# Top-k attention and a cosine-gated feed-forward on one core: four weight chunks in each of the first units, some in other buffers, and twelve units instead of eight transposed by TensorE

## The chip, the core and the metric

The kernel runs on one core of a Trainium2 chip. The metric is the device time of one execution in microseconds; three executions of the kernel before took 1467.22, 1468.61 and 1470.07 us. The core has five engines with a queue of instructions each: TensorE (PE in the profile; PEld are its weight loads), VectorE (DVE), ScalarE (ACT), GpSimd (POOL) and SyncE (SP), which only issues DMAs here. They wait for each other by semaphores.

## The reference

```python
# q, k, v: (8, 8, 576, 64): 8 batches, 8 heads
scores = 0.125 * q @ k.T
kth = np.partition(scores, -32, axis=-1)[..., -32:-31]
scores = np.where(scores >= kth, scores, -1e9)
attn = softmax(scores)              # the sum has 1e-9 added
x = (attn @ v).transpose(0, 2, 1, 3).reshape(4608, 512)
h = x @ w_in                        # (512, 2048)
return (h * np.cos(h)) @ w_out      # (2048, 512)
```

Both weight matrices arrive as 64-bit floats.

## The kernel before

**Units.** The 4608 tokens are cut into 36 blocks of 128; a block with two heads is a unit, so that there are 144 units, four to a block. Where a block spans two batches its units have two parts. For each unit, TensorE makes the scores of 128 queries against 576 keys for two heads (`scores`, L223); ScalarE copies them into SBUF (`take_scores`, L233 and L234). VectorE finds the 32 largest of each row: it folds the row into 288 larger values (`fold_high`, L244) and 288 lesser ones, and searches both with MAX8 and MATCH_REPLACE8 (L349, L354) in four rounds, of which the fourth takes the lesser values too (`topk_round`). The lesser values come from VectorE at once (`fold_now`, L252) in units up to number `EARLY`, and from two integer operations of GpSimd (`fold_sum` L262, `fold_low` L271) after it. From the bound found, ScalarE masks (`mask`, L378 and L380) and exponentiates with row sums (`exponentials`, L388); VectorE adds and inverts the sums (`sums` and `reciprocal`, L396 and L401; the tiles `den` and `rden`).

**Two ways to transpose.** The weights of attention must be transposed before they meet `v`. In early units GpSimd normalises them (`normalise`, L409), TensorE transposes them in nine pieces (`transposes_now`, tile `tp`), ScalarE copies the result into `pT`, TensorE multiplies with `v` (`values`, L474) and ScalarE copies the product into the block's `xT` (`take_values`, L485). In paired units GpSimd splits the words into 16-bit halves (`split`, L421 and L423), SP writes them to HBM and reads them back through a transposing DMA, and VectorE normalises the product (L483) two units at a time.

**Feed-forward.** When a block's four units are done, eight steps `ff1` (L534) multiply its `xT` by `w_in`; ScalarE evacuates each bank of two steps twice (`take_first`, L548 and L550), GpSimd and ScalarE make the cosine (L570, L579, and `sines`, L589, whose function and that of the exponentials need different tables, so that a table load stands at each change), GpSimd multiplies (`gate`, L596), and eight steps `ff2` (L609) multiply by `w_out`. `feed(n)` puts up to n such steps into TensorE's order, under a credit of five a slot less 0.9 for each unit whose scores are made there. There are 576 steps in all.

**Weights.** They are loaded in 32 chunks of 512 KB and converted to 32-bit floats in three stages: `decode_first` on ScalarE (L128), `decode_second` on GpSimd (L138) and VectorE (L141), `decode_third` on GpSimd (L151). Chunks are staged in seven buffers with the tag `g`, which the feed-forward's gates use too; the four buffers with the tag `x` belong to the sines.

**The order.** It is written out by hand: one slot for each unit, in which the functions are called in a fixed order, and each call appends instructions to the queues of its engines. Slots up to `EARLY` = 8 are `early_slot`, then come `slot` and, for the last units, `last_slot`. In slot i, VectorE searches unit i, the mask, exponentials and transposes are of unit i - 1, and scores are made ahead. The early slot reads the sums in its third round, the other in its fourth:

```python
        decode_second(n)                  # early_slot
        topk_round(u, 2, both(w))
        topk_round(u, 3)
        if w:
            normalise(w)
...
        decode_second(2)                  # slot
        topk_round(u, 3, both(w), z)
```

Of the kernel before, what the change touches and what calls it, by code (L numbers as in the profile page):

```python
# [11 lines left out]
I32 = mybir.dt.int32  # L12
# [5 lines left out]
P = 128  # L18
# [12 lines left out]
def kernel(  # L31
# [16 lines left out]
    NP = H // 2  # L48
# [12 lines left out]
    ffw = ctx.enter_context(tc.tile_pool(name="ffw", bufs=2))  # L61
# [13 lines left out]
    CW = 512  # L75
# [8 lines left out]
    for i in range(DF // CW):  # L84
        w = consts.tile([P, NC, CW], F32, tag=f"w_in{i}", name=f"w_in{i}")
# [4 lines left out]
    for f in range(NF):  # L90
        w = consts.tile([P, DM], F32, tag=f"w_out{f}", name=f"w_out{f}")
        w_out.append(w)
        chunks.append((moe_w_out[f * P : (f + 1) * P, :], w))
    CHUNKS, XB = 7, 4
    ff = {"live": 0, "tick": 0, "now": 0, "credit": 0.0, "end": False, "kind": 0, "half": 0, "open": 0}

    wq = {"next": 0, "loaded": deque(), "second": deque(), "third": deque(), "done": 0, "ready": 0}

    def staged():
        return sum(len(wq[k]) for k in ("loaded", "second", "third"))  # L100

    def load_weights(n):
        for _ in range(n):
            i = wq["next"]
            if i >= len(chunks):
                return
            src, dst = chunks[i]
            if not DECODE:
                nc.sync.dma_start(out=dst, in_=src)
                wq["next"] = wq["done"] = i + 1  # L110
                continue
            if staged() + ff["live"] >= CHUNKS:
                return
            st = ffw.tile([P, CW, 2], I32, tag="g", name="st", bufs=CHUNKS)
            nc.sync.dma_start(out=st.rearrange("p w i -> p (w i)"), in_=src)
            wq["loaded"].append((st, dst))
            wq["next"] = i + 1


# [2 lines left out]
    def decode_first(n):  # L122


        for _ in range(min(n, len(wq["loaded"]))):
            st, w = wq["loaded"].popleft()
            hi = st[:, :, 1]
            nc.scalar.activation(  # L128
                out=w, in_=hi.bitcast(F32), func=AF.Prelu, scale=2.0**-111, alpha=2.0**32
            )  # L130
            wq["second"].append((st, w))

    def decode_second(n):

        for _ in range(min(n, len(wq["second"]))):
            st, w = wq["second"].popleft()
            wi, lo = w.bitcast(I32), st[:, :, 0]
            nc.gpsimd.tensor_scalar(  # L138
                out=lo, in0=lo.bitcast(U32), scalar1=2.0**-29, scalar2=1.0, op0=ALU.mult, op1=ALU.mult
            )  # L140
            nc.vector.tensor_scalar(  # L141
                out=wi, in0=wi, scalar1=3, scalar2=None, op0=ALU.logical_shift_left
            )
            wq["third"].append((st, w))

    def decode_third():

        while wq["third"]:
            st, w = wq["third"].popleft()
            wi = w.bitcast(I32)  # L150
            nc.gpsimd.tensor_tensor(out=wi, in0=wi, in1=st[:, :, 0], op=ALU.add)  # L151
            wq["done"] += 1
# [16 lines left out]
    NU = len(units)  # L169
# [68 lines left out]
    def fold_high(u):  # L238

        s, sc = u["s"], u["sc"]  # L240
        if u["n"] > EARLY:
            del u["sc"]
        u["rest"] = work.tile([P, 2, S], F32, tag="rest", name="rest", bufs=1)
        nc.vector.tensor_tensor(  # L244
            out=u["rest"][:, :, HS:S], in0=sc[:, :, 0:HS], in1=s[:, :, HS:S], op=ALU.max
        )
# [9 lines left out]
    def fold_sum(u):  # L256

        if not u["folds"]:
            return
        s = u["s"].bitcast(I32)  # L260
        u["low"] = work.tile([P, 2, HS], F32, tag="low", name="low", bufs=1)
        nc.gpsimd.tensor_tensor(  # L262
            out=u["low"].bitcast(I32), in0=s[:, :, 0:HS], in1=s[:, :, HS:S], op=ALU.add
        )

    def fold_low(u):

        if not u["folds"]:
            return
        low = u["low"].bitcast(I32)  # L270
        nc.gpsimd.tensor_tensor(  # L271
            out=low, in0=low, in1=u["rest"][:, :, HS:S].bitcast(I32), op=ALU.subtract
        )
# [15 lines left out]
    def topk_first(u, w):  # L289

        u["top"] = tops[u["n"] % len(tops)]
        merges = w and w["folds"]
        if merges:
            merge_first(w)
        if u["folds"]:
            if u["n"] > EARLY:
                fold_sum(u)
            fold_high(u)
        else:
            u["rest"] = work.tile([P, 2, S], F32, tag="rest", name="rest", bufs=1)  # L300
        if merges:
            merge_second(w)
        if u["folds"] and u["n"] <= EARLY:
            fold_now(u)
        topk_round(u, 0, [lambda: bounds(w), lambda: distances(w)] if w else ())

# [27 lines left out]
    def merge_first(u):  # L334
        n = TOPK // 2 + 1
        u["lesser"] = u["top"].rearrange("p j r i -> p j (r i)")[:, :, 2 * n : 3 * n]
        nc.vector.tensor_reduce(
            out=u["lesser"], in_=u["top"][:, :, 0:n], axis=mybir.AxisListType.X, op=ALU.min
        )

    def merge_second(u):
        nc.vector.tensor_reduce(
            out=u["top"][:, :, TOPK - 1, 1], in_=u.pop("lesser"), axis=mybir.AxisListType.X,
            op=ALU.max,
        )
# [57 lines left out]
    def both(u):  # L403
        return [lambda: sums(u), lambda: reciprocal(u)] if u else ()
# [88 lines left out]
    for w in widths:  # L493
# [10 lines left out]
    second = deque(  # L504
        (blk, i, f) for blk in blocks for i in range(blk["w"] // P) for f in range(0, NF, 2)
    )
# [159 lines left out]

    EARLY, LAST = 2 * NP, NU - NP
    scored, last, last_values = {}, {}, {}  # L670
    for i, u in enumerate(units):
        two = i % 2 == 0 and EARLY + 2 < i < LAST + 2 and (len(u["parts"]) == 1 or u["hp"] == 0)
# [4 lines left out]
    at_slot = {}  # L677
    order = [(b, hp) for b in range(B) for hp in range(NP)]
    for n in range(NP, len(order)):
        i = last[order[n - 5]] if n >= 5 else 0  # L680
        at_slot.setdefault(max(i, NP + 2), []).append((load_qk, *order[n]))
        i = last_values[order[n - 6]] if n >= 6 else 0
        at_slot.setdefault(max(i + 4 - i % 2, NP + 2), []).append((load_v, *order[n]))

    for hp in range(NP):
        at_slot.setdefault(hp, []).append((load_v, 0, hp))
# [7 lines left out]
        u["paired"] = EARLY <= i < LAST  # L694

    def early_slot(i, u, w):
        n = 3 if i < 6 else 2
        topk_first(u, w)
        if i == 0:
            decode_second(1)  # L700
        scores(units[i + 1])
        for load, b, hp in at_slot.get(i, []):
            load(b, hp)
        load_weights(n)
        if w:
            mask(w)
            exponentials(w)
        topk_round(u, 1)

        decode_second(n)  # L710
# [4 lines that stand above are left out]
        take_banks()  # L715
        take_scores(units[i + 1])
        gate(1)
        decode_third()
        feed(2)
        reduce_first()  # L720
        reduce_second()
        if i != NP:
            decode_first(n - 1)
        if w:
            transposes_now(w)
        feed(1)
        decode_first(n - len(wq["second"]))
        if w:
            values([w])
            take_values([w])  # L730
        feed(2)
        sines(2)

    def send(x):

        split(x)
        write_halves(x)
        transposes(x)

    def slot(i, u, w, x, z):  # L740
        load_weights(2)
        if x:
            send(x)
        topk_first(u, w)
        fold_low(u)
        topk_round(u, 1)
        topk_round(u, 2)
        made = scored.get(i, [])
        if z:
            take_banks()  # L750
        feed(1)

        for m in made:
            scores(m)
        if z:
            values(z)


        late = len(made) > 0

        decoding = i < EARLY + 8
        if i % 2 and not decoding:
            sines(1)
        if w:
            mask(w)
        take_banks()
        if w and late:
            exponentials(w)
        take_scores(units[i + 1])
        if w and not late:  # L770
            exponentials(w)
        decode_second(2)
        topk_round(u, 3, both(w), z)
        for load, b, hp in at_slot.get(i, []):
            load(b, hp)
        gate(1)
        feed(1 if len(made) == 2 else 2)
        take_banks()
        decode_third()
        decode_first(2)  # L780
        reduce_first()
        reduce_second()
        feed(1 if len(made) == 2 else 3)
        if decoding or i == LAST:
            sines(1)
# [50 lines left out]
    for i in range(NU + 1):  # L836
# [4 lines left out]
        u, w = (units[i - n] if 0 <= i - n < NU else None for n in range(2))  # L841
        x = units[i - 2] if EARLY <= i - 2 < LAST else None
# [54 lines left out]
```

## Time and profile before

| | |
|---|---|
| median of three runs | 1468.61 us |
| the profiled execution | 1468.61 us, of which its span is 1466.8 us |
| granted TensorE clock, mean | 0.97 |
| busy: PE, DVE, ACT, POOL | 1404.1, 1365.5, 1078.5, 1160.0 us |
| start of slots 0, 9, 13, 22 (their L244) | 7.38, 108.29, 153.79, 242.49 us |
| moved by DMA | 229.53 MB, mean 156 GB/s |

A slot is counted from the start of its L244 on VectorE. From slot 22 two slots take 18.69 us; in slots 2 to 5 one takes 10.8 us. Busy times of TensorE are modelled, and a busy share is a mean over stages. Idle time of an engine that isn't the bound in its stage costs nothing by itself. The granted clock is 0.5 in stretches of the first 167 us and 1.0 from there to the end.

### The profile page before, as it was taken

How to read it: one execution, taken by the hardware profiler on the slowest of the kernel's cores; microseconds unless marked ns; L12 is line 12 of the kernel's file. 1: busy time of each engine (PE TensorE's matmuls, PEld its weight loads, DVE VectorE, ACT ScalarE, POOL GpSimd, SP SyncE). 2: the span in 40 equal slices, each digit the busy share in tenths (PEclk: the TensorE clock that was granted, in tenths of full speed). 3: DMA queues.
4: the chain of work that ended last, by engine and by line, in shares of the span. 5: the costliest groups of instructions: out<-in, count | busy, mean ns of one | idle time of the engine just before them, and what ended most of it. 6: DMA issues, size and time to landing. Idle time of an engine off the chain costs nothing.

```text
span 1466.8 us, 30361 instructions
## 1 busy us (share of the span) xinstructions
PE 1404.1 (96%) x10360; PEld 1012.0 (69%) x10360; DVE 1365.5 (93%) x5209; ACT 1078.5 (74%) x1908; POOL 1160.0 (79%) x836
## 2 busy tenths in 40 slices
PE   4778899999999999999999999999999999999998
PEld 3566567777777767777777767777677777777765
DVE  7999999999999999999999999999999999999831
ACT  4667677777777777777777777777777787777651
POOL 4679888888888887888888888888888888888410
PEclk6578999999999999999999999999999999999999
DMA  8434576666665566557665667666766566655200
GB/s 279 152 101 130 151 199 175 159 162 174 184 166 151 152 186 180 167 145 180 192 167 146 150 172 193 168 151 162 192 179 152 149 161 175 168 151 147 67 8 15
DMA packets 405547, 229.53 MB, mean 156 GB/s; under 512 B 355088, under 2 KB 371728, under 8 KB 405392
## 3 DMA queue, kind: packets, MB, share of 16 engines
q1 hardware_dynamic: 399984, 217.93, 56.3%
q10 hardware_dynamic: 5408, 9.65, 1.8%
q8 instruction: 82, 1.34, 0.4%
q14 instruction: 73, 0.60, 0.1%
HBM read 45.09 MB, written 95.94 MB: 96 GB/s over the span
## 4 chain that ended last, share of the span: by engine, by line
PE 84%; DVE 7%; ACT 5%; DMA 2%; POOL 1%; issue 1%; SPq 0%; ACTq 0%; POOLq 0%
PE mm L534 31%; PE o L609 31%; PE rim L474 11%; PE sc L223 7%; DVE top L349 3%; PE rim L223 2%; DVE rest L354 2%; ACT s L388 1%; ACT s L380 1%; PE tp L448 1%; DMA st<-in_moe_w_in_dram 1%; ACT s L233 1%; ACT L388 1%; DMA v<-in_v_dram 0%; DVE w_out L141 0%
## 5 line engine op out<-in xcount | busy, mean ns | idle before, releaser
L534 PEld LDWEIGHTS mm<-xT,w_in 128*128 128x128 f32 x4608 | 537.1, 192 | 68.7 <-issue 65.7
L609 PE MATMUL o<-w_out,g 128*128 128x512 f32 x1152 | 541.8, 604 | 11.4 <-POOL g L596 8.7
L534 PE MATMUL mm<-xT,w_in 128*128 128x128 f32 x4608 | 539.7, 275 | 1.1 <-DVE xT L483 0.8
L349 DVE MAX8 top<-rest 128x8 f32<-128x288 f32 x1148 | 481.3, 454 | 0.0
L421 POOL COPY halves<-s 128x2304 uint16<-128x2304 uint16 x132 | 277.7, 2104 | 150.2 <-ACT s L388 147.0
L354 DVE MATCH_REPLACE8 rest<-top,rest 128x288 f32<-128x288 f32 (+1 forms) x860 | 377.0, 446 | 0.0
L609 PEld LDWEIGHTS o<-w_out,g 128*128 128x128 f32 x1152 | 203.8, 192 | 201.3 <-issue 187.0
L349 DVE MAX8 top<-low 128x8 f32<-128x288 f32 x568 | 239.3, 448 | 2.7 <-POOL low L271 2.7
L388 ACT ACTIVATE s<-s,nd 128x576 f32<-128x576 f32 x288 | 220.1, 766 | 0.8
L380 ACT ACTIVATE s<-s,top 128x576 f32<-128x576 f32 x288 | 206.1, 766 | 0.0
L271 POOL TENSOR_TENSOR low<-low,rest 128x576 int32<-128x576 int32 x133 | 187.9, 1413 | 10.4
L262 POOL TENSOR_TENSOR low<-s 128x576 int32<-128x576 int32 x133 | 187.8, 1412 | 1.3 <-DVE rden L401 1.3
L548 ACT ACTIVATE g<-mm 128x512 f32<-128x512 f32 x144 | 85.8, 596 | 130.5 <-PE mm L534 126.4
L474 PE MATMUL rim<-pT,v 128*64 128x128 f32 (+1 forms) x2560 | 161.9, 271 | 8.6 <-ACT pT L455 8.0
L579 POOL TENSOR_TENSOR x<-g,x 128x1024 f32<-128x1024 f32 x68 | 160.9, 2366 | 5.7
L596 POOL TENSOR_TENSOR g<-g,x 128x1024 f32<-128x1024 f32 x68 | 161.4, 2374 | 2.6 <-ACT x L589 2.5
L223 PE MATMUL sc<-k,q 64*128 64x448 f32 (+1 forms) x640 | 155.3, 589 | 8.3 <-DMA k<-in_k_dram 8.3
L474 PEld LDWEIGHTS rim<-pT,v 128*64 128x64 f32 x2560 | 134.3, 140 | 20.4 <-ACT pT L455 10.4
L233 ACT COPY s<-sc 128x896 f32<-128x896 f32 x144 | 129.2, 897 | 4.5 <-PE sc L223 4.1
L354 DVE MATCH_REPLACE8 low<-top,low 128x288 f32<-128x288 f32 x284 | 123.5, 442 | 0.0
L234 ACT COPY s<-rim 128x256 f32<-128x256 f32 x144 | 55.0, 382 | 87.4 <-PE rim L474 87.4
L244 DVE TENSOR_TENSOR rest<-sc,s 128x576 f32<-128x576 f32 x142 | 106.2, 748 | 6.6 <-ACT s L234 6.6
(59 smaller groups left out, 1325.6 us busy)
## 6 DMA issues: line engine op xcount, KB each, us to landing
rows<-halves SPq DMA_DIRECT2D x132, 640.0 KB, 3.0
out_dram<-ob ACTq DMA_DIRECT2D x36, 256.0 KB, 2.1
q<-in_q_dram SPq DMA_DIRECT2D x31, 288.0 KB, 3.8
st<-in_moe_w_in_dram SPq DMA_DIRECT2D x16, 512.0 KB, 5.6
v<-in_v_dram SPq DMA_DIRECT2D x32, 256.0 KB, 3.3
st<-in_moe_w_out_dram SPq DMA_DIRECT2D x16, 512.0 KB, 4.1
k<-in_k_dram SPq DMA_DIRECT2D x31, 144.0 KB, 3.7
k<-in_k_dram SPq DMA_DIRECT2D x32, 128.0 KB, 3.8
```

What stands on the lines that cost most here:

```text
L223: nc.tensor.matmul(to[r0 : r0 + rows, j, 0 : k1 - k0], st["q"][d, q0 : q0 + rows], st["k"][d, k0:k1], start=True, stop=True,)
L262: nc.gpsimd.tensor_tensor(out=u["low"].bitcast(I32), in0=s[:, :, 0:HS], in1=s[:, :, HS:S], op=ALU.add)
L271: nc.gpsimd.tensor_tensor(out=low, in0=low, in1=u["rest"][:, :, HS:S].bitcast(I32), op=ALU.subtract)
L349: nc.vector.max(to[:, j], src[:, j])
L354: nc.vector.match_replace(rest[:, j], to[:, j], src[:, j], NEG)
L380: nc.scalar.activation(out=s[:, j], in_=s[:, j], func=AF.Prelu, bias=less[:, j, 1:2], scale=1.0, alpha=FAR)
L388: nc.scalar.activation(out=s[:, j], in_=s[:, j], func=AF.Exp, bias=nd[:, j : j + 1], scale=SCALE, accum_out=den[:, j, 0:1],)
L421: nc.gpsimd.tensor_copy(out=halves[:, :, 0 : 2 * S], in_=s.rearrange("p (k h) -> p h k", h=2))
L474: nc.tensor.matmul(o[d, to], lhsT, rhs, start=c == 0, stop=c == NT)
L534: nc.tensor.matmul(mm[:, at : at + w], w_in[f // FC][:, c, (f % FC) * P : (f % FC + 1) * P], blk["xT"][:, c], start=c == 0, stop=c == NC - 1,)
L596: eng.tensor_tensor(out=g, in0=g, in1=x, op=ALU.mult)
L609: nc.tensor.matmul(o, g[:, at : at + P], w_out[f], start=f == 0, stop=f == NF - 1)
```

## The change

An early slot handles four weight chunks in slots 0 to 7 and two after them, instead of three up to slot 5. A chunk with an odd number among the first twelve is staged in a buffer of the sines' tag `x`, up to four at a time; the limit of seven on the others counts only those with the tag `g`. `EARLY` is 12 instead of 8, so slots 9 to 12 become early slots, and units 8 to 11 are normalised by GpSimd and transposed by TensorE. A new name, `DECODING` = 8, keeps the old place for what else hung on `EARLY`: units up to number 8 have their lesser values from VectorE, those after it from GpSimd. The first loads of the second batch move from slot 6 to slot 10. The slots in which the sines stand at the end of `slot` are now those before 14 instead of 16.

```diff
-    def staged():
-        return sum(len(wq[k]) for k in ("loaded", "second", "third"))
+    def staged(spare=0):
+        return sum(c[2] == spare for k in ("loaded", "second", "third") for c in wq[k])
...
-            if staged() + ff["live"] >= CHUNKS:
+            spare = i < 3 * XB and i % 2 == 1 and staged(1) < XB
+            if spare:
+                st = ffw.tile([P, CW, 2], I32, tag="x", name="st", bufs=XB)
+            elif staged() + ff["live"] >= CHUNKS:
                 return
-            st = ffw.tile([P, CW, 2], I32, tag="g", name="st", bufs=CHUNKS)
+            else:
+                st = ffw.tile([P, CW, 2], I32, tag="g", name="st", bufs=CHUNKS)
             nc.sync.dma_start(out=st.rearrange("p w i -> p (w i)"), in_=src)
-            wq["loaded"].append((st, dst))
+            wq["loaded"].append((st, dst, int(spare)))
...
-        if u["n"] > EARLY:
+        if u["n"] > DECODING:
             del u["sc"]
...
-            if u["n"] > EARLY:
+            if u["n"] > DECODING:
                 fold_sum(u)
...
-        if u["folds"] and u["n"] <= EARLY:
+        if u["folds"] and u["n"] <= DECODING:
             fold_now(u)
...
-    EARLY, LAST = 2 * NP, NU - NP
+    EARLY, LAST, DECODING = 3 * NP, NU - NP, 2 * NP
...
-        at_slot.setdefault(max(i, NP + 2), []).append((load_qk, *order[n]))
+        at_slot.setdefault(max(i, DECODING + 2), []).append((load_qk, *order[n]))
...
-        at_slot.setdefault(max(i + 4 - i % 2, NP + 2), []).append((load_v, *order[n]))
+        at_slot.setdefault(max(i + 4 - i % 2, DECODING + 2), []).append((load_v, *order[n]))
...
     def early_slot(i, u, w):
-        n = 3 if i < 6 else 2
+        n = 4 if i < 8 else 2
         topk_first(u, w)
+        if i > DECODING:
+            fold_low(u)
...
-        decoding = i < EARLY + 8
+        decoding = i < EARLY + 2
```

The other changed lines carry the third member of a chunk's entry through the stages of the decoding.

More of the change, by code (lines that the diff above doesn't have):

```diff
@@ L125, in decode_first @@
         for _ in range(min(n, len(wq["loaded"]))):
-            st, w = wq["loaded"].popleft()
+            st, w, spare = wq["loaded"].popleft()
             hi = st[:, :, 1]
@@ L130, in decode_first @@
             )
-            wq["second"].append((st, w))
+            wq["second"].append((st, w, spare))
     def decode_second(n):
         for _ in range(min(n, len(wq["second"]))):
-            st, w = wq["second"].popleft()
+            st, w, spare = wq["second"].popleft()
             wi, lo = w.bitcast(I32), st[:, :, 0]
@@ L143, in decode_second @@
             )
-            wq["third"].append((st, w))
+            wq["third"].append((st, w, spare))
     def decode_third():
         while wq["third"]:
-            st, w = wq["third"].popleft()
+            st, w, _ = wq["third"].popleft()
             wi = w.bitcast(I32)
```

## The prediction

> **What bounds the kernel now.** I read the stage windows first, cut at starts of slots (a slot begins with the L244 fold on VectorE), then VectorE's waits up to slot 22, then ScalarE's timeline at slot 9. Columns of the windows: busy us and count by engine, granted TensorE clock, DMA share, GB/s. The five rows are slots 0-8, 9-12, 13-21, 22-139 and the end.
>
> ```profile
> 7.38:108.29 100.91, 62.30 (x412) 49.37 (x412) 95.98 (x344) 64.22 (x138) 64.40 (x68) 0.65 0.55 175
> 108.29:153.79 45.50, 39.72 (x242) 27.21 (x242) 43.33 (x151) 31.50 (x58) 42.69 (x35) 0.88 0.49 143
> 153.79:242.49 88.70, 82.52 (x628) 57.12 (x628) 83.04 (x324) 64.56 (x113) 72.94 (x51) 0.96 0.62 168
> 242.49:1353.03 1110.54, 1109.89 (x8403) 801.82 (x8402) 1090.21 (x4250) 863.37 (x1504) 950.07 (x650) 1.00 0.64 167
> ```
>
> In slots 0-8 VectorE is busy 95.98 of 100.91 us and TensorE only 62.30: VectorE bounds. From slot 22 TensorE is never idle (1109.89 of 1110.54) and bounds, at 18.69 us a pair of slots; VectorE needs 9.38 + 9.09 = 18.47. Between, both are near full.
>
> ```profile
> DVE den L396 <- ACT s L388: 6.7, 6, 2.4
> DVE rest L244 <- ACT s L234: 6.6, 2, 6.3
> DVE top L349 <- POOL low L271: 2.7, 1, 2.7
> DVE xT L483 <- ACT s L234: 2.1, 1, 2.1
> ```
>
> (waited for: total us, times, longest; 7 to 243 us). ScalarE's instructions in order of time from 111 us (start, length):
>
> ```profile
> 111.07 0.27 ACT L485 COPY xT<-rim 128x128 f32<-128x128 f32 x1 [1.93 <-PE rim L474]
> 111.36 1.28 ACT L589 ACT_TABLE_LOAD   x1
> 112.65 2.19 ACT L589 ACTIVATE x<-x,halfpi 128x1024 f32<-128x1024 f32 x2
> 114.75 0.19 ACT L378 ACTIVATE nd<-nd 128x2 f32<-128x2 f32 x1
> 114.84 1.42 ACT L380 ACTIVATE s<-s,top 128x576 f32<-128x576 f32 x2
> 116.28 1.28 ACT L388 ACT_TABLE_LOAD   x1
> 117.58 0.78 ACT L388 ACTIVATE s<-s,nd 128x576 f32<-128x576 f32 x1
> ```
>
> VectorE's most frequent wait is `den`: the row sums come from ScalarE's exponentials. In slot 9 (from 108.29) mask and exponentials stand behind two sines and two table loads, so that `den` comes 10.95 us into the slot. In `slot()` `den` is read in the last round, 1.06 us before the slot's end, so only 1.9 us are lost. In `early_slot` it is read in round 2, with 4.6 us of search still to follow (slot 5: 69.08 to 73.71).
>
> [...] `nd` was ready at 110.0, its L378 ran at 114.75 behind the sines. [...] an L141 shift, else 0.42, took 2.57 us from 126.32 while GpSimd's L596 ran from 126.20 to 128.61.
>
> **The change part by part.** Sizes come from this one execution: span 1466.8, 1468.6 with what lies around it, which is the median shown. The instruction order of the built program is the same again on every engine from slot 22, with equal amounts of feed-forward work left, so I need only the start of slot 22 and what TensorE has in hand there.
>
> *1. Four chunks.* The program loads 4, 4, 4, 4, 3, 4, 1, 4, 1 chunks in slots 0-8 (before: 3 each up to slot 5, then 2), and the last is decoded in slot 10 instead of 12. A chunk costs VectorE 0.34 (start to start of L141), ScalarE 0.58, GpSimd 0.75 + 1.25. GpSimd's 7.17 busy in a slot of 10.8 grow to 9.2: hidden. SP's queue gets two more loads ahead, and the loads of pairs and values behind them land about 2 us later, before they are needed. But ScalarE now waits in slot 0 for a fourth chunk: the third landed at 22.25, the three are 1.3 to 3.2 us apart, the fourth lands at about 24.1; unit 0's mask stands behind it: +1.85 for slot 1. The same queue makes +1.15 in slot 2; 0.34 each in slots 3 and 4; nothing in 5 and 6 (`den` is late by 2.4 there anyway); -0.5 in slot 7 with one chunk fewer, +0.7 in slot 8, where three decodes stand ahead of the copies of the transpose. **Sum +3.9**; bounds +1.7 (five more shifts alone) and +5.
>
> *2. Nothing starts earlier for it.* The order has five and three first-layer steps in slots 5 and 6 and the first second-layer steps in slot 9, as before: tokens and gates hold them, not weights.
>
> The first loads of batch 1 move from slot 6 to slot 10; they are read in slot 14, and took some 7 us from first issue to last landing (63.42 to 70.08 for the pair): no cost. The folds of units 9 to 12 stay on GpSimd (L262, L271), 2.8 us a slot, before and after.
>
> *3. Slot 9 as an early slot.* The sines of slot 8 stay ahead of the mask. `den` at 10.9 as before, then 4.6 us: 15.6 instead of 12.0. **+3.6.** What is queued behind: GpSimd's normalise (L409) now waits for `rden`, and the gate stands behind it, at 13.1 instead of 5.6 us into the slot; TensorE's next second-layer step waits for that gate, and the values of unit 8 stand behind the step. They end at about 18.7, 3.1 us into slot 10.
>
> *4. Slots 10-12.* Removed: split for four units (GpSimd 4 x 2.5), four L483 (VectorE 4 x 0.2), four writes and four transposing DMAs on SP. Added: TensorE 4 x 1.15 of transposes, GpSimd 8 x 0.74, ScalarE 4 x 1.5 of copies. [...] But early slots are a closed loop: values, xT (0.3), a pending evacuation (1.3), mask and exponentials (3.4), `den` to `rden` (0.6), normalise (1.5), transposes (1.15), one feed step (1.8), values (1.3). With values of unit 8 ending 3.1 into slot 10, `den` comes at 8.3, and the slot lasts 8.3 + 4.6 = 12.9. TensorE's list in slot 10 and 11 is four steps of 1.8, scores 1.3, transposes 1.15, values 1.3: 11, plus its wait for normalise. I get 12.9, 12.8 and 11.0: 36.7 instead of 11.87 + 9.78 + 11.85 = 33.5. **+3.2**; bounds -3.5 (10.0 a slot) and +5.
>
> *5. Slots 13-15.* Slot 13 has five first-layer steps in a row; their evacuations (1.3 each) and slot 13's and 14's sines with table loads stand ahead of the exponentials of slots 14 and 15: up to 12.1 and 11.7 instead of 12.2 (a late `low`, 2.7, which goes) and 9.1. Between 0 and +2.5 for the three; **+1.5**.
>
> *6. Slots 16-21.* 58.4 before, of which VectorE needs 56. Slot 18's wait for `k` (landed at 207.42) stays, since its load is issued in slot 17 as before. **-1.0.**
>
> *7. From slot 22.* In slots 20 and 21 TensorE has four steps instead of eight. Before, its scores began 2.7 us into slot 22; they can begin 0.8 into it. Those 1.9 us come back at 18.69 - 18.47 = 0.22 a pair. **-1.9.**
>
> Sum: 3.9 + 3.6 + 3.2 + 1.5 - 1.0 - 1.9 = **+9.3**: 1477.9 us.
>
> **The rivals.**
>
> A, *faster*: the waits of the middle vanish. VectorE needs 120 us for slots 9-21 (13 x 9.09, a few L483 and L141) and took 134.2. If `den` is never over 1 us late in slots 9 to 12, the collisions (3.9), slot 9's wait (1.9) and slot 14's late `low` (2.7) go, against 3.9 lost at the start, and with step 7: -6.5, about 1462. For it: TensorE had gaps of 4.1, 1.3 and 4.6 us there. Against it: the sines' place ahead of the mask, which the order keeps. It decides where the exponentials end within 5.5 us of a slot's start.
>
> B, *no change*: the start costs only the five shifts (+1.7), slot 9 is as I say (+3.6), but the loop of slots 10-12 runs at 10.0 a slot (-3.5): with step 7 about 1468.5. For it: at full clock the loop without evacuation and normalise's second half is about 9.7.
>
> C, *worse*: TensorE, idle up to the gate in slot 9, falls to the half clock (it held it for 6.8 us from 115.7) and late values of unit 8 push on each slot after: +4, about 1482.
>
> That the change doesn't do what it says: the fourth chunk is there in six of the eight slots, and the twelfth transpose too, so this is out.
>
> **How the numbers follow.** The likeliest case has 0.70, C 0.07, A 0.13 and B 0.10. The likeliest one's own range is 1472 to 1484: about half of the way to the lower bounds of steps 1, 4 and 5, and to the upper ones. The range of 8 in 10 reaches down over B to 1466.5. About 0.2%, 2.9 us, can be told from no change: faster 0.13 (A), same 0.10 (B), slower 0.77.
>
> **What would show it.** Slot starts of the changed kernel near 112 (slot 9), 128 (10) and 164 (13), against 108.3, 120.3 and 153.8; a `den` wait of over 4 us in slot 9; the gate at slot 9 behind L409's counterpart and TensorE waiting for it; no long shift in slots 11 and 12; slot 22 near 254. A start of slot 10 before 122, or of slot 13 before 154, would make it wrong, and so would a loss that arises after slot 22.

## The result: 1.1% slower, and the profile after

| | before | changed |
|---|---|---|
| median | 1469.13 us (4 runs, 1467.22 to 1470.07) | 1484.72 us (4 runs, 1482.91 to 1486.47) |
| ratio | | 1.0108, 95% interval 1.009 to 1.0125 |
| profiled execution, its span | 1468.61, 1466.8 us | 1485.72, 1483.9 us |
| start of slots 9, 10, 13, 16, 22 | 108.29, 120.30, 153.79, 184.14, 242.49 | 114.23, 129.81, 169.70, 202.77, 260.78 |

The direction was forecast; the size was not. The change cost 15.6 us between the medians where 9.3 was forecast, and 1484.72 lies 0.7 us above the upper end of the range, 1484.0.

First the windows of the changed kernel, cut like those of before at slots 0, 9, 13, 22, 140 and the end:

```profile
7.42:114.23 106.81, 62.90 (x412) 50.17 (x412) 100.26 (x349) 68.36 (x144) 74.26 (x78) 0.65 0.60 190
114.23:169.70 55.47, 47.38 (x303) 33.93 (x304) 38.79 (x145) 29.49 (x61) 30.85 (x28) 0.87 0.01 1
169.70:260.78 91.08, 84.06 (x624) 57.03 (x622) 82.87 (x322) 66.22 (x119) 73.92 (x50) 1.00 0.60 158
260.78:1368.87 1108.09, 1107.29 (x8381) 800.78 (x8382) 1090.12 (x4250) 861.90 (x1502) 946.80 (x648) 1.00 0.62 166
1368.87:1483.90 115.03, 106.08 (x662) 73.93 (x660) 52.63 (x138) 52.44 (x94) 28.03 (x22) 0.99 0.11 33
```

The second row carries the result. Slots 9 to 12 took 55.47 us instead of 45.50, while VectorE's work there shrank from 43.33 to 38.79 and GpSimd's from 42.69 to 30.85. Two engines were relieved and the stage became longer: the amount of work of neither sets its pace. TensorE's busy time rose from 39.72 to 47.38 us. Its mean clock, 0.87 after 0.88, looks unchanged but belongs to a longer stretch: half clock for 2 x 0.13 x 55.47 = 14.4 us, against 2 x 0.12 x 45.50 = 10.9. The first row is 5.9 us longer, the third 2.4. From slot 22 the kernel is slightly shorter.

VectorE's waits between 7 and 280 us (waited for: total us, times, longest):

```profile
DVE den L400 <- ACT s L392: 28.8, 12, 5.5
DVE rest L248 <- ACT s L238: 6.9, 3, 6.4
DVE w_in L145 <- ACT w_in L132: 0.9, 2, 0.7
DVE xT L487 <- ACT s L238: 0.7, 2, 0.4
```

In the same stretch of the kernel before, `den` took 7.2 us in all; it takes 28.8 now. The late `low` (2.7) has gone, as forecast, and so has the one long wait for a copy (2.1). And ScalarE in slot 9 (start, length), from 2.8 us after its start:

```profile
117.02 0.27 ACT L489 COPY xT<-rim 128x128 f32<-128x128 f32 x1 [2.50 <-PE rim L478]
117.30 1.28 ACT L593 ACT_TABLE_LOAD   x1
118.59 2.19 ACT L593 ACTIVATE x<-x,halfpi 128x1024 f32<-128x1024 f32 x2
120.69 0.19 ACT L382 ACTIVATE nd<-nd 128x2 f32<-128x2 f32 x1
120.78 1.43 ACT L384 ACTIVATE s<-s,top 128x576 f32<-128x576 f32 x2
122.23 1.28 ACT L392 ACT_TABLE_LOAD   x1
123.52 0.77 ACT L392 ACTIVATE s<-s,nd 128x576 f32<-128x576 f32 x1
```

It is the same sequence as before, 5.94 us later in time and the same 10.95 us into the slot when `den` is read at 125.18. What differs is where VectorE reads it: in round 2, after a wait of 5.5 us.

### The profile page after: what moved, and what is told of

It reads as the page before. It is cut to its first block, busy times and chain, and to the rows that moved or that the text cites. A ratio compares the mean times of both kernels' runs of the same rounds, so it can differ in the third digit from the quotient of the medians.

```text
span 1483.9 us, 30423 instructions
## 1 busy us (share of the span) xinstructions
PE 1412.7 (95%) x10396; PEld 1019.8 (69%) x10396; DVE 1364.9 (92%) x5205; ACT 1080.9 (73%) x1922; POOL 1155.7 (78%) x836
## 4 chain that ended last, share of the span: by engine, by line
PE 88%; ACT 4%; DVE 4%; DMA 2%; POOL 1%; issue 0%; SPq 0%; ACTq 0%; POOLq 0%
PE mm L538 33%; PE o L613 33%; PE rim L478 11%; PE sc L227 8%; PE rim L227 2%; DVE top L353 2%; DVE rest L358 1%; ACT s L392 1%; ACT s L384 1%; PE tp L452 1%; DMA v<-in_v_dram 1%; DMA k<-in_k_dram 1%; DMA st<-in_moe_w_in_dram 0%; DMA q<-in_q_dram 0%; ACT L392 0%
## 5 line engine op out<-in xcount | busy, mean ns | idle before, releaser
L425 POOL COPY halves<-s 128x2304 uint16<-128x2304 uint16 x128 | 269.3, 2104 | 149.2 <-ACT s L392 147.5
L275 POOL TENSOR_TENSOR low<-low,rest 128x576 int32<-128x576 int32 x133 | 187.7, 1411 | 10.4
L583 POOL TENSOR_TENSOR x<-g,x 128x1024 f32<-128x1024 f32 x68 | 160.9, 2366 | 5.7
L248 DVE TENSOR_TENSOR rest<-sc,s 128x576 f32<-128x576 f32 x142 | 106.2, 748 | 6.9 <-ACT s L238 6.9
## 6 DMA issues: line engine op xcount, KB each, us to landing
k<-in_k_dram SPq DMA_DIRECT2D x32, 128.0 KB, 3.5
```

The costliest lines, as they stand in the source:

```text
L275: nc.gpsimd.tensor_tensor(out=low, in0=low, in1=u["rest"][:, :, HS:S].bitcast(I32), op=ALU.subtract)
L425: nc.gpsimd.tensor_copy(out=halves[:, :, 0 : 2 * S], in_=s.rearrange("p (k h) -> p h k", h=2))
L583: nc.gpsimd.tensor_tensor(out=x, in0=g, in1=x, op=ALU.subtract)
```

## The experiments

Ratios are to the kernel before, run beside each on the same chip; one per cent is 14.7 us. The changed kernel itself stands at 1.0108. Slots count from L248 (L244 in kernels made from before).

**The two parts apart.** `chunks_only` is the changed kernel with eight early slots again; `units_only` is the kernel before with twelve, and three chunks.

```diff
# chunks_only, against the changed kernel
-    EARLY, LAST, DECODING = 3 * NP, NU - NP, 2 * NP
+    EARLY, LAST, DECODING = 2 * NP, NU - NP, 2 * NP
...
-        decoding = i < EARLY + 2
+        decoding = i < EARLY + 8
```

```diff
# units_only, against the kernel before
-    EARLY, LAST = 2 * NP, NU - NP
+    EARLY, LAST, DECODING = 3 * NP, NU - NP, 2 * NP
...
+        if i > DECODING:
+            fold_low(u)
...
-        decoding = i < EARLY + 8
+        decoding = i < EARLY + 2
```

In both, the loads of batch 1 stand where the change's parts want them (slot 6 in the first, slot 10 in the second).

> Four chunks a unit and the spare buffers, but eight units transposed by TensorE as before. Theory (the start pays for the chunks, the middle gives it back): slot 9 starts near 114.2 as in the changed kernel (before: 108.3), slot 9 lasts 12.0 again, and slots 10 to 12 are shorter than before's 33.5 by up to 5.6[...]; end 0 to +4 us against before. Rival (weights held the feed-forward back): first steps start earlier and the end is over 3 us below before.

> Twelve units transposed by TensorE, three chunks as before. Theory (the two parts add up): slot 9 starts at 108.3 as before, lasts 15.6, slots 10 to 12 take 39 to 40, slot 22 starts near 255, and the end is +9 to +12 us against before. Rival (the early slots 9 to 12 lose only because of the four chunks ahead of them): slot 10 to 12 take under 35, end within 4 us of before.

Measured: `chunks_only` 1469.90 us, ratio 1.0012 (1.0005 to 1.0019), about +1.8 us; `units_only` 1486.36 us, ratio 1.0128 (1.0106 to 1.015), about +18.8 us. `chunks_only` ended where its theory had it, but its slots 10 to 12 took 33.1 us and not up to 5.6 less than 33.5. (Of the 5.6, 3.9 are the excess of shifts of before, rival A's collisions: one took 2.57 us from 126.32 instead of 0.42, and two from 147.59 took 2.55 together instead of 0.76, beside work of GpSimd; 1.7 are five shifts of 0.34.) `units_only` had the slots as its theory said (15.6, then 39.8), but the loss was nearly twice the +9 to +12 expected. So the loss is that of the four units, and the chunks, a small loss alone, take some 2.9 us off it. The intervals of units and both overlap, so the size of that help isn't firm. Its place can be looked for in the windows of the middle, slots 9 to 12 and 13 to 21, of `chunks_only`:

```profile
113.77:158.87 45.10, 40.43 (x258) 28.99 (x259) 39.59 (x147) 30.08 (x54) 40.68 (x29) 0.92 0.31 88
158.87:245.56 86.69, 80.70 (x613) 56.80 (x612) 83.00 (x324) 61.85 (x110) 65.14 (x47) 0.96 0.65 173
```

and of `units_only`:

```profile
109.64:165.05 55.41, 47.26 (x303) 33.88 (x304) 42.87 (x148) 33.55 (x68) 38.77 (x36) 0.87 0.22 69
165.05:266.39 101.34, 87.80 (x624) 59.08 (x622) 83.22 (x323) 66.39 (x119) 75.58 (x52) 0.97 0.54 142
```

With the chunks alone, slots 9 to 12 last 45.10 us against 45.50 before; with the units alone 55.41, which is the changed kernel's 55.47. What the chunks buy stands in the next row: with three a slot, slots 13 to 21 last 101.34 us, with four 91.08. But that profiled execution of `units_only` was 4.9 us over its median, so up to half of the difference may belong to the execution. In return the chunks lengthen slots 0 to 8, by 5.9 us in the changed kernel's profile.

**Where `den` is read.** `den_late` reads it in the last round in slots 9 to 12.

```diff
-        topk_round(u, 2, both(w))
-        topk_round(u, 3)
+        topk_round(u, 2, both(w) if i <= DECODING else ())
+        topk_round(u, 3, both(w) if i > DECODING else ())
```

> The changed kernel with the row sums of slots 9 to 12 read in the fourth round instead of the third. Theory (VectorE's early read of the sums costs once what stands behind it, and the closed loop from values over xT, exponentials, normalise and transposes sets the pace after it): slot 9 lasts 12.0 instead of 15.6, slots 10 to 12 still about 39 to 40 together since the loop is unchanged, slot 13 starts 3.5 us earlier (166.2), end -3.5 against the changed kernel. Rival (TensorE's amount of work sets slots 9 to 12, wherever the sums are read): slot 13 and the end within 1 us of the changed kernel. Second rival (each of the four slots loses by the read): slot 13 earlier by 8 or more.

Measured: 1485.40 us, ratio 1.0113 (1.0096 to 1.013): nothing gained. Slot 9 did shrink from 15.6 to 12.0 us, and slot 13, counted from the start of slot 9, began 3.2 us earlier, about as the theory had it. But slots 10 to 13 lasted 15.6, 12.3, 12.3 and 13.1, and from the start of slot 9 to that of slot 16 it is 88.58 us, in the changed kernel 88.54. TensorE's order in time is the same: its values in slot 11 begin 32.91 us after the start of slot 9, in the changed kernel 32.87. VectorE's waits for `den` in slots 9 to 12 fell from 16.5 us to 8.0, the longest from 5.5 to 2.9, without changing the end: VectorE isn't the pace of slots 9 to 12. On the end the rival was right.

**TensorE's idle time and clock in slot 9.** `fill` keeps TensorE busy with transposes of the identity ahead of unit 8's transposes, which overwrite them; nothing else changes. `fill_long` is the same with 40 instead of 20.

```diff
         tp = ps.tile([P, 2, 512], F32, tag="sc", name="tp", bufs=2)
+        if u["n"] == DECODING:
+            for _ in range(20):
+                nc.tensor.transpose(tp[:, 0, 0:P], ident, ident)
```

> The changed kernel with 20 transposes of the identity on TensorE ahead of the transposes of unit 8, so that TensorE does not idle in slot 9 while it waits for normalise; they write a tile that the real ones overwrite. Theory (idling in slot 9 brought the half clock from 125.5 to 135.7, which slowed four second-layer matmuls by 1.9 and the values by 1.1 on the loop): slot 10 lasts 12.2 instead of 15.1, everything after 2.9 us earlier. Rival (the clock is off the path, the gate on GpSimd and the sums set slot 10): slot 10 within 0.5 us of 15.1.

This one missed. 1482.83 us, ratio 1.0093 (1.0074 to 1.0111), slot 10 at 14.7 us instead of 15.1. The twenty covered 2.35 us of the wait, and the clock fell all the same, from 128.0 to 134.8. The rival's length of slot 10 came true, but since the clock had fallen it says nothing on what the clock costs.

`gate_only` moves slot 9's gate ahead of normalise on GpSimd; `gate_fill` does so with 34 extra transposes.

```diff
+        if i == DECODING + 1:
+            gate(1)
         normalise(w)
...
-        gate(1)
+        if i != DECODING + 1:
+            gate(1)
```

> The changed kernel with, in slot 9 alone, the gate ahead of normalise on GpSimd, and 34 transposes of the identity on TensorE in its wait for normalise. Theory (slot 10 is long because the second-layer step stands behind the gate, that behind normalise, and TensorE idles into the half clock): the step follows the transposes at once at full clock (1.98 for four matmuls instead of 3.78), the values of unit 8 end near 131.2 instead of 135.9, slot 10 lasts about 10.5 instead of 15.1, and the end is -4 to -5. Rival (the wait only moves, and TensorE's list pays it back in slots 11 to 13): end within 1 us of the changed kernel.

> The gate of slot 9 stands ahead of normalise on GpSimd, without the extra transposes. Theory (the half clock makes most of slot 10's excess): TensorE still idles some 4 us up to normalise, so the half clock still falls; the second-layer step (3.8 us) starts 0.9 us sooner, right behind the transposes, and the values of unit 8 end some 5.2 us into slot 10 instead of 6.1; slot 10 lasts 14.0 to 15.0 us and the kernel stays within 0.2 per cent of the changed one: ratio to before 1.009 to 1.011. Rival (the order of gate and normalise is what counts, the clock comes with it): slot 10 lasts 10.4 to 11.5 us and the ratio is 1.0077 as with the filler.

> Forty extra transposes instead of twenty ahead of unit 8's, the gate still behind normalise. They cover the wait for normalise whole, and leave the gap of about 1.5 us ahead of the second-layer step. Theory (the half clock makes most of slot 10's excess, and a gap of 1.5 us after a busy stretch doesn't bring it): step and values run at full clock (1.9 and 1.3 us), the values of unit 8 end some 3.2 us into slot 10, slot 10 lasts about 12.2 us instead of 15.1, and the ratio to before is about 1.0085. Rival (the late gate is what counts, or the gap of 1.5 us alone brings the half clock): slot 10 stays at 14 us or more, ratio 1.009 to 1.011.

| | gate | transposes | slot 10 | ratio |
|---|---|---|---|---|
| changed | after normalise | 0 | 15.1 us | 1.0108 (1.009 to 1.0125) |
| `fill_long` | after normalise | 40 | 12.2 us | 1.0082 (1.0069 to 1.0095) |
| `gate_only` | before it | 0 | 12.8 us | 1.0091 (1.0077 to 1.0106) |
| `gate_fill` | before it | 34 | 10.4 us | 1.0077 (1.0063 to 1.0091) |

TensorE in the changed kernel, from slot 9 into slot 10 (in brackets: idle time, and what ended it):

```profile
118.93 3.84 PE L538 MATMUL mm<-xT,w_in 128*128 128x128 f32 x32
126.76 1.11 PE L452 MATMUL tp<-ident,s 128*128 128x128 f32 x4 [4.00 <-POOL s L413]
...
129.81 3.78 PE L613 MATMUL o<-w_out,g 128*128 128x512 f32 x4 [0.87 <-POOL g L600]
133.52 1.98 PE L478 MATMUL rim<-pT,v 128*64 128x128 f32 x16
135.28 0.61 PE L478 MATMUL rim<-pT,v_tail 128*64 128x128 f32 x4
```

In `fill_long`:

```profile
122.33 4.53 PE L451 MATMUL tp<-ident 128*128 128x128 f32 x40
126.70 0.60 PE L455 MATMUL tp<-ident,s 128*128 128x128 f32 x4
...
128.61 1.98 PE L616 MATMUL o<-w_out,g 128*128 128x512 f32 x4 [0.77 <-POOL g L603]
130.53 1.09 PE L481 MATMUL rim<-pT,v 128*64 128x128 f32 x16
131.45 0.39 PE L481 MATMUL rim<-pT,v_tail 128*64 128x128 f32 x4
```

And in `gate_only`:

```profile
126.22 1.11 PE L452 MATMUL tp<-ident,s 128*128 128x128 f32 x4 [3.97 <-POOL s L413]
...
128.19 3.62 PE L613 MATMUL o<-w_out,g 128*128 128x512 f32 x4
131.74 1.12 PE L478 MATMUL rim<-pT,v 128*64 128x128 f32 x16
```

The same four matmuls of the second layer take 3.78 us in the first and 1.98 in the second, the first sixteen of the values 1.98 and 1.09. The granted clock says why. These are the windows from 126.8 to 131.7 us, its column the third from the end, of the changed kernel and of `fill_long`:

```profile
126.80:131.70 4.90, 4.03 (x12) 2.59 (x13) 4.87 (x19) 1.24 (x3) 4.90 (x4) 0.50 0.00 0
```

```profile
126.80:131.70 4.90, 4.13 (x34) 2.55 (x32) 4.87 (x20) 1.24 (x3) 4.90 (x4) 1.00 0.00 0
```

For `fill_long` the theory hit: 12.2 us forecast and measured. With the gate in its old place, the clock alone is worth 2.9 us in slot 10. For `gate_only` both missed (14.0 to 15.0, or 10.4 to 11.5; it came to 12.8): the half clock fell, but the step stood right behind the transposes and the clock was back from about 131.8, so that the values ran at full speed. Gate and clock together are worth 4.7 us. In `gate_fill` TensorE has no gap from 117 us to the end of slot 10, at 137.9, and slot 10 takes 10.4 us, as forecast.

**A bank taken late.** In slots 9 to 12, `banks_early` emits the pending evacuation of a first-layer step ahead of the transposes, not behind the copy of `xT`.

```diff
+        if i > DECODING:
+            take_banks()
         transposes_now(w)
```

> The changed kernel with one more evacuation of full banks ahead of the transposes in slots 9 to 12. Theory (TensorE's own list sets the pace of 12.3 us there, and 1.44 us of it is its wait for a bank whose evacuation stands on ScalarE behind the copy of the values): the gap of 1.44 before the first-layer step after the values goes, slots 11 and 12 last 11.0 instead of 12.4, slot 14 starts 4 us earlier, end -3 to -5 against the changed kernel. Rival (ScalarE's mask and exponentials set the pace): slots 11 and 12 within 0.4 of 12.4.

Measured: 1478.44 us, ratio 1.0085 (1.0065 to 1.0104), the end as forecast. Of the two slots named, slot 12 fell to 10.8 us and slot 11 stayed at 12.5; slot 10 fell instead, from 15.1 to 13.3, and why was not shown. TensorE's cycle in the changed kernel, from one unit's values to the next's (slot 11):

```profile
147.10 1.09 PE L478 MATMUL rim<-pT,v 128*64 128x128 f32 x16
148.02 0.39 PE L478 MATMUL rim<-pT,v_tail 128*64 128x128 f32 x4
149.85 2.05 PE L538 MATMUL mm<-xT,w_in 128*128 128x128 f32 x16 [1.44 <-ACT x L554]
151.83 1.02 PE L227 MATMUL sc<-k,q 64*128 64x448 f32 x4
152.69 0.39 PE L227 MATMUL rim<-k,q 64*128 64x128 f32 x4
153.01 2.05 PE L538 MATMUL mm<-xT,w_in 128*128 128x128 f32 x16
154.90 1.88 PE L613 MATMUL o<-w_out,g 128*128 128x512 f32 x4
...
157.60 1.88 PE L613 MATMUL o<-w_out,g 128*128 128x512 f32 x4
159.41 1.09 PE L478 MATMUL rim<-pT,v 128*64 128x128 f32 x16
```

and in `banks_early`:

```profile
144.59 1.09 PE L478 MATMUL rim<-pT,v 128*64 128x128 f32 x16
145.52 0.39 PE L478 MATMUL rim<-pT,v_tail 128*64 128x128 f32 x4
145.84 2.05 PE L538 MATMUL mm<-xT,w_in 128*128 128x128 f32 x16
...
155.39 1.09 PE L478 MATMUL rim<-pT,v 128*64 128x128 f32 x16
```

The cycle is 159.41 - 147.10 = 12.31 us, and 10.80 without the gap of 1.44. In the transposes, left out above, TensorE has no wait at all: it does not stand for normalise.

**Fewer steps.** `fewer_feeds` leaves one of the four feed-forward steps out of slots 9 to 12; it comes later.

```diff
-        feed(2)
+        if i <= DECODING:
+            feed(2)
```

> The changed kernel with at most three feed-forward steps instead of five in each of slots 9 to 12; the steps left out are made in slots 13 to 21, and from slot 22 the order is the same. Theory (TensorE's list of four steps, transposes and values sets 12.3 us a slot): slots 11 and 12 fall to 9.5 to 10.5, slot 13 starts 5 to 8 us earlier, and since TensorE has room in slots 16 to 21 (they last 9.0 to 9.9 at VectorE's pace) the end is -4 to -7 against the changed kernel. Rival (feed-forward work can only be moved): slots 13 to 21 lengthen by as much, end within 1.5 us.

Measured: 1480.76 us, ratio 1.0078 (1.0062 to 1.0093). Slots 11 and 12 took 10.4 and 9.5 us instead of 12.5 and 12.3, as forecast. TensorE's cycle, from the values at 142.59 to those at 151.99, is 9.40 us instead of 12.31: a step of 1.9 left the list, and the wait for a bank went with it. Part was given back, since slots 17 and 18 grew from 9.0 and 9.8 to 12.7 and 12.4, with a wait of 3.6 us for a late `low` and one of 2.9 for a copy.

**All together.** `all_fixes` joins `gate_fill`, `banks_early` and `den_late`.

> The changed kernel with three edits at once: in slot 9 the gate ahead of normalise and 34 filling transposes, one more evacuation of banks ahead of the transposes in slots 9 to 12, and the sums of these slots read in the fourth round. Theory (TensorE's list is the one pace of slots 9 to 13, and the edits take 4.7 and three or four times 1.44 off it): slots 10 to 12 take about 32 instead of 39.9, slot 13 starts 8 to 9 us earlier, the end is -8 to -11 against the changed kernel and still +4 to +7 against before (the start, and the transposes themselves). Rival (the savings of the single edits overlap): -5 to -6, as with one of them.

Measured: 1476.14 us, ratio 1.0037 (1.0024 to 1.0051), some 10.4 us below the changed kernel, as forecast. Slots 9 to 12 took 44.9 us, less than the 45.5 before. They don't lengthen the kernel any more. Slots 0 to 8 still cost 4 us, and slots 13 to 15 took 34.7 us instead of 30.4.

**The sines.** `sines_mid` moves `sines(2)` from the end of an early slot to just behind the taking of the scores; `before_sines` does the same to the kernel before.

```diff
         take_scores(units[i + 1])
+        sines(2)
...
-        sines(2)
```

> The changed kernel with the sines of an early slot after the copies of the scores instead of at its end. Theory (two sines and a table load ahead of the mask make the sums of slot 9 late): the sums' wait of 5.5 in slot 9 falls to 2 to 3.5, slot 9 lasts 12 to 13.5 instead of 15.6, later slots start that much earlier, end -2 to -3.5. Rival (TensorE's list sets slots 9 to 12 whenever the sums come): end within 1 us of the changed kernel.

> The kernel before with the same move of the sines. Theory: the exponentials of unit 8 end some 1.7 us earlier, the sums' wait of 1.9 in slot 9 goes, and with it 1.5 to 2 us of the start of slot 10; at the end -1 to -2 against before, as far as TensorE's reserve doesn't take it up. Rival (slot 9's wait is hidden by TensorE's waits after it): within 0.5 us of before.

Both theories missed. `sines_mid`: 1481.25 us, ratio 1.0097 (1.0081 to 1.0113), slot 9 still 15.5 us. `before_sines`: 1472.34, ratio 1.0034 (1.0022 to 1.0045), slower than before, slot 9 at 14.9 us. The move did more than was meant: the sines being ready sooner, second-layer steps stand ahead in TensorE's list. In `before_sines`:

```profile
114.22 1.98 PE L474 MATMUL rim<-pT,v 128*64 128x128 f32 x16
115.98 0.46 PE L474 MATMUL rim<-pT,v_tail 128*64 128x128 f32 x4
116.37 5.42 PE L609 MATMUL o<-w_out,g 128*128 128x512 f32 x12
121.72 1.02 PE L223 MATMUL sc<-k,q 64*128 64x448 f32 x4
```

Three steps, 5.42 us, now stand between the values and the next scores, and VectorE's fold of slot 10 waits 2.1 us for the copy of those. What the sines' place alone is worth can't be read from these two.

**The chunks at less cost.** `chunks_later` is `chunks_only` with three chunks in slots 0 to 2 and four in slots 3 to 7. `three` is `chunks_only` with three in slots 0 to 8, and the spare buffers used only from chunk 15 on; it was meant to beat both kernels.

```diff
# chunks_later
-        n = 4 if i < 8 else 2
+        n = 3 if i < 3 else 4 if i < 8 else 2
# three
-            spare = i < 3 * XB and i % 2 == 1 and staged(1) < XB
+            spare = 15 <= i and i % 2 == 1 and staged(1) < 2
...
-        n = 4 if i < 8 else 2
+        n = 3 if i < 9 else 2
```

> Four chunks a unit in slots 3 to 7 alone, three before, eight units transposed by TensorE. Theory (the fourth chunk in slots 0 to 2 costs the waits of 2 to 3 us for DMA[...]): slots 1 and 2 as before (11.9, 10.8), slots 4 to 6 0.7 longer, slot 9 starts near 111 instead of 113.8, end -2 to -3 against the kernel with four chunks from the start, about -1 against before. Rival (slot 9's start is taken up later anyway): end within 0.5 us of the kernel with four chunks from the start (+1.8 against before).

> Three chunks a unit up to slot 8 (before: up to 5), odd chunks from the fifteenth staged in the sines' buffers, two at a time, eight units transposed by TensorE. From slot 9 its order of feed-forward steps is that of the kernel with four chunks, which made up 5 us between slots 9 and 22. Theory (early decoding helps the middle, the fourth chunk alone costs the start): slots 0 to 5 as before, slot 9 starts within 1.5 us of 108.3, slot 22 near 240 to 241 instead of 242.5, end -1 to -3 against before. Rival (staging in the sines' buffers makes the first sines or loads wait): slot 9 or 10 longer by over 2, end at or above before.

Measured: `chunks_later` 1469.81 us, ratio 1.0000 (0.9991 to 1.0009); `three` 1468.93, ratio 0.9998 (0.9986 to 1.0011). `chunks_later` begins slot 9 at 110.18, 3.6 us before `chunks_only`, and 2.4 of that it has by slot 3 (42.02 against 44.46): in these executions the fourth chunk was dear in slots 0 to 2. Its end, some 1.8 us below `chunks_only`, lies between what theory and rival said. `three` beats the changed kernel but only equals the one before, so its forecast of -1 to -3 missed. Its rival's cause isn't seen either: slots 9 and 10 take 12.1 and 11.8 us, as before.

## Why the prediction was right in sign and short in size

Each term, as the profiled executions have it: length of the slots after, less that before.

| step | forecast | measured |
|---|---|---|
| 1, slots 0-8 | +3.9 | +5.9 |
| 3, slot 9 | +3.6 | +3.6 |
| 4, slots 10-12 | +3.2 | +6.4 |
| 5, slots 13-15 | +1.5 | +2.7 |
| 6, slots 16-21 | -1.0 | -0.3 |
| 7, from slot 22 | -1.9 | -1.2 |
| sum | +9.3 | +17.1 (spans 1466.8 and 1483.9) |

The sum is 1.5 us more than the medians differ: the profiled execution of before was 0.5 under its median, that of the changed kernel 1.0 over it.

**Step 3 was exact**: `den` at 10.95 us, a slot of 15.6. Rival A asked for exponentials by 5.5 us into the slot, and the trace has them end at 10.9. But `den_late` adds what the step didn't say: this 3.6 isn't a cost of its own. TensorE's list needs the time anyway, and a slot 9 without the wait makes slots 10 to 13 longer.

**Step 4 failed: it cost 6.4 us, twice the 3.2 forecast.** Slots 10 to 12 were put at 12.9, 12.8 and 11.0 us and took 15.1, 12.5 and 12.3. Two parts of the step are wrong.

The first is the half clock. The step put one second-layer step at 1.8 and the values at 1.3 us, full clock, and the end of unit 8's values at 3.1 us into slot 10. They took 3.78 and 2.37 us and ended at 135.89, 6.1 into it. The mechanism had been written down as rival C, +4 us with a chance of 7 in 100; and the kernel before shows the half clock for 6.8 us from 115.7, in slots 9 and 10. It belonged in the likeliest case, since step 3 itself had TensorE wait for the gate up to 13.1 us into the slot. With `fill_long` the clock stays, slot 10 takes 12.2 us (forecast for the changed kernel: 12.9), and the kernel gains 0.26% between the ratios, 3.8 us, with intervals of the two that overlap a little. C's half clock is shown, and its 1482 is the nearest of the four ends. That it pushes on each slot after is not: slots 11 and 12 last 12.5 and 12.3 us in `fill_long` too.

The second is the loop. The step closed it over `den`, normalise, transposes and values. (Its terms up to `den` in slot 10 add up to 8.1 us and not the 8.3 given, and the 12.8 of slot 11 isn't worked out from them.) The traces show no wait of TensorE for normalise in slots 11 and 12; its own list is the loop. Summed from the rows above: values 1.3, a wait for a bank 1.44, two first-layer steps 3.9, scores 1.2, two second-layer steps 3.5 and transposes 1.0, from start to start, together 12.3 us, which is the length of slots 11 and 12 (12.5 and 12.3). The step had 11 for the list "plus its wait for normalise". That wait is nil, and the wait for a bank, worth 1.44, stood in no step. Two experiments bear this out: `banks_early` takes the gap away and the cycle falls by 1.5, `den_late` halves VectorE's waits and nothing falls. That slot 11 was forecast at 12.8 and took 12.5 is no support for the loop that was argued; slot 12 at 11.0 was wrong by 1.3. In slot 10 the trace shows TensorE keep to the order of its list: the last copy for unit 8's values ended at 130.22, but they began at 133.52, behind the second-layer step that had waited for its gate. So the sum over the list was a first lower bound of the slot, and I should have put the bank wait into it.

**Step 1 was short by 2.0, and much of that is the execution.** Eight experiments have the changed kernel's slots 0 to 8; their slot 9 begins at 111.76 to 114.64, in half of them by 112.4, which is +4.1 against the one profile of before. So the +3.9 was about right as a sum, by luck, since its parts were off both ways; the changed kernel's 114.23 is a late one. In it, slot 1 grew by 0.85 us, less than the 1.85 forecast, as the fourth chunk landed at 23.33, not 24.1. Slot 2 grew by 2.1 instead of 1.15, with a wait of 1.3 us for `den`. Slots 3 and 4 each grew by 0.68 instead of 0.34, and there the cause is in view. Slot 3 of the changed kernel:

```profile
47.95 2.20 POOL L142 TENSOR_SCALAR st<-st 128x512 int32<-128x512 uint32 x3
49.23 1.87 DVE L145 TENSOR_SCALAR w_in<-w_in 128x512 int32<-128x512 int32 x4
```

and the same place before:

```profile
46.04 1.08 DVE L141 TENSOR_SCALAR w_in<-w_in 128x512 int32<-128x512 int32 x3
```

Three shifts took 1.08 us, four take 1.87: 0.79 more where 0.34 was charged. The second of the four lasts 0.87 us instead of 0.42, from 49.56 to 50.43, just as GpSimd's last L142 runs (49.43 to 50.15); the second of slot 2 lasts 0.87 too, where all twelve of the kernel before in slots 1 to 4 take 0.41 or 0.42. The fourth chunk has made GpSimd's work and VectorE's meet: before, GpSimd's last L138 of slot 3 ended at 44.89 and the shifts began at 46.04. Step 1 did count GpSimd's longer list but called it hidden; its cover, that the two engines don't meet, was gone. The prediction had read such an overlap from L141 beside the gate (2.57 us instead of 0.42), and did not look for one with this pair. No run here tried slot 3 with L142 moved off, so the cause is read from the overlap and not shown. In slot 7 the forecast -0.5 came out at +0.7, with a shift of 1.69 us beside GpSimd's L583 (95.90 to 98.25). Slots 5 and 6 grew by 0.4 and 0.7 instead of nothing, and slot 8 shrank by 0.4 instead of growing by 0.7.

**Step 5** was 1.2 us over its forecast and 0.2 over its upper bound. The cause named was there: `den` waits of 3.1 and 1.6 us at 191.02 and 202.07, behind evacuations and sines. **Step 6**: slot 21 took 10.97 us instead of 9.5, with a `den` wait of 1.9; the gain was smaller for it. **Step 7**: up to slot 141 the changed kernel got back 2.5 us, a little over the 1.9; its tail was 1.3 us longer. In that tail the clock averages 0.91 over a stretch of 20 us; in the execution of before it stays at 1.00 there, and `chunks_only`, which has no loss to speak of, has such a stretch too (tail 105.7 us). So I put that part down to the execution rather than to the change.

**What stays of 15.6 us.** By the ratios, `all_fixes` takes 10.4 of it away and leaves 5.4, about the start (its slot 9 begins 4.0 us late) and slots 13 to 15. `gate_fill` and `banks_early` alone take 4.6 and 3.4. How the remaining 2.4 divides between `den_late`, which gave nothing alone, and their meeting isn't settled.

## What to carry to other kernels

Before a loop through several engines is priced, add up the in-order list of each engine for one cycle, with every buffer wait in it: a wait seen on VectorE can vanish without gain when TensorE's list has the same length, as 8.5 us of `den` waits did in `den_late`. Where an edit makes TensorE idle for a few microseconds, price the work behind the gap at the half clock in the likeliest case, if the trace already shows it falling there; here, behind 4.00 us of idle time and another 0.87, four matmuls took 3.78 us instead of 1.98. Where a trace shows an instruction lengthened beside another engine's work, as a shift of 2.57 us instead of 0.42 beside the gate, one more instruction each can bring together what never met before; slot 3, with 0.87 us instead of 0.42, looks like such a case.

## What the runs showed of the hardware

The clock fell some time after TensorE's last matmul: that ended at 122.77 in the changed kernel and the clock was down from 125.5; in `gate_only` 122.25 and 125.0: 2.7 to 2.8 us. The half clock lasted 6.8 us in the kernel before (from 115.7), in `gate_only` (from 125.0) and in `fill` (from 128.0), 10.2 in the changed kernel (from 125.5), and 3.4 in that one's tail (from 1388.4): once, twice and three times 3.4. The full clock ahead of the fall had lasted 3.4 us in the kernel before (from 112.3) and 6.8 in the changed one (from 118.7). In the changed kernel the 3.4 us ahead of the fall (122.1 to 125.5) held 0.7 us of matmuls, so TensorE was not idle throughout. Those of `fill` (124.6 to 128.0) held 1.4, and the clock still fell; in slot 12 of the changed kernel, those around the gap of 1.44 (159.6 to 163.0) held 2.0, and the clock stayed.

The gap's length alone doesn't decide. In the changed kernel's tail a gap of 1.92 us ended at 1387.79 and the clock was down from 1388.4; at the same place of before one of 1.93 ended at 1371.96, and the clock stayed at 1.00. In the changed kernel it stayed past a gap of 2.59 (253.46 to 256.05), and was down from 262.0 behind the next, of 2.37 (to 261.58); in `fill` it was down from 128.0 behind one of 2.16 (124.38 to 126.54). A gap of 0.77 in `fill_long` did not bring it down. What decides beside the length was not shown.

That forty extra transposes, 4.5 us of work of no use, take 2.9 us off a slot (15.1 to 12.2) was new to me; in the whole kernel it is 0.26% between the ratios, whose intervals overlap a little.
